# Pooled attention followed by four experts: the first batch's scores by halves of the tokens, chunk 0 written out anew, batch 1 turned by TensorE

## The chip, the cores and the metric

The kernel runs on one core of one Trainium2 chip. The metric is the device time of one execution in microseconds. Six runs of the kernel before are given with their median, and one further trace shows where its time goes, instruction by instruction.

## The reference

Eight batches of eight heads, 576 tokens, head width 64. Keys and values are first averaged over groups of eight tokens (72 pooled keys); every query attends to the 72. The eight heads of a token, side by side, are a row of 512 numbers; 4608 such rows go through four experts of hidden width 1024, whose outputs are added with weights that depend on the row.

```python
k_p = k.reshape(B, H, Sp, pool, D).mean(axis=3)      # pool = 8, Sp = 72
v_p = v.reshape(B, H, Sp, pool, D).mean(axis=3)
attn = softmax(q @ k_p.T / sqrt(D))
x = (attn @ v_p).transpose(0, 2, 1, 3).reshape(B * S, H * D)
p = domain_probs / domain_probs.sum(-1)
for e in range(4):
    out += p[:, e:e+1] * (relu(x @ w1[e]) @ w2[e])
```

## The kernel before

**Chunks.** Every batch gives one chunk of 512 tokens (chunks 0 to 7); the last 64 tokens of all eight batches make chunk 8 (`rem_*`). Chunk 0 is multiplied plainly: `up` (L446) makes hidden blocks `fc` 0 to 7 of an expert, and experts 1 and 2 go down by `down_plain` (L599), expert 0 by `down`. All chunks after it use a scheme with seven products in place of eight for both layers: `up_product` (L493, seven steps for each of two halves, "units") and `down` (L561, seven steps). It needs sums of weights (`first_weight_sums` for w1, `weight_sums` for w2), of inputs (`x_sum`) and of hidden blocks (`hidden_sums`), all made by VectorE through `combine` (L187).

**Order.** Every engine runs its instructions in the order in which the program states them; nothing is reordered. From chunk 1 on a loop runs over slots g. In a slot stand one step of `up_product` for unit 0, the step before it for unit 1, and one step of `down` for the expert before; seven slots make one expert of one chunk. The pieces of attention for the next batch (`fold_keys`, `queries`, `keys`, `scores`, `context`, `turn`), its loads and its `x_sum` pieces stand at slots written by hand in `pieces_later` (L714); for batch 2, slots 0 to 27 run under chunk 1, for batch 3 slots 28 to 55 under chunk 2. Batch 1's pieces stand in `pieces_first` (L681), between the blocks of chunk 0. Where TensorE has nothing to do early on, `idle` (L252) issues matmuls on zeros.

**Loads.** `load_part` brings a quarter of a batch's keys and values at a time and adds it to the quarters before it in memory (L115), `load_whole` brings everything (batches 0 and 1), `load_q` the queries. Most loads are issued by GpSimd and converted on the way, so they queue behind each other on GpSimd and on its DMA queue (q0); an issue also waits for the landing of the load eight issues before it. The queries of batch 0 come as two plain loads from SyncE (queue q1, L132) into `acc`, and VectorE and ScalarE convert them (L136). GpSimd also adds one product of `down` to `acc` for experts 1 to 3 (L592, step 4 of `down`).

**Turning.** What attention gives has tokens on partitions; the experts need the 512 features there. `turn` (L338) does this for 128 tokens at a time: for batch 0 by four TensorE transposes and a ScalarE copy out of PSUM (L348, L349), for all others by a DMA transpose from SyncE's queue (L344). Queries and keys of batches 0 and 1 are turned by TensorE (L285, L233), later ones by DMA (L277, L227).

**PSUM.** `att` and `att_first` are pairs of banks for attention, taken in turn; `unit10` and `unit11` hold hidden blocks; `o_ps0` and `o_ps1` hold the products of `down`. An access to a bank by one engine waits for the access of another engine to the same bank that stands before it in the program.

**Last expert.** `down_last` (L623) makes four quarters of the output in four banks, each of two blocks of 128 tokens; `add` (L642) multiplies a block by its weight and adds it to `acc`, and `store` sends a quarter.

Of the kernel before, what the change touches and what calls it, by code (L numbers as in the profile page):

```python
# [12 lines left out]
BF16 = mybir.dt.bfloat16  # L13
# [4 lines left out]
def kernel(  # L18
# [57 lines left out]
    gate_at = const.tile([1, NR], BF16, name="gate")  # L76
# [27 lines left out]
    def load_whole(b, src, nm):  # L104

        room = wt_bf[:, 1:E].rearrange("p e s i d -> p (e s i d)")
        at = {"kraw": 0, "vraw": 1}[nm] * H * POOL * D
        raw = room[0:SP, at:at + H * POOL * D].rearrange("j (h r d) -> j h r d", h=H, r=POOL)
        for hs in groups(b):
            nc.gpsimd.dma_start(  # L110
                out=raw[:, hs], in_=src[b, hs].rearrange("h (j r) d -> j h r d", r=POOL)
            )
        raws[(nm, b)] = raw
# [9 lines left out]
    def load_q(b):  # L123
        q_sb = raws[("q", b)] = qpool.tile([P, H, NR, D], BF16, name="q_sb")
        src = q[b, :, 0:NT, :].rearrange("h (p r) d -> p h (r d)", r=NR)
        if b:
            nc.gpsimd.dma_start(out=q_sb[:].rearrange("p h r d -> p h (r d)"), in_=src)
            return

        wide = acc[:].rearrange("p r (g t) -> p (r g) t", t=NR * D)  # L130
        for hs in groups(b):
            nc.sync.dma_start(out=wide[:, hs], in_=src[:, hs])  # L132
        for pair in range(NPAIR):
# [110 lines left out]
    def sum_keys(hs):  # L244
        kp = sum_pool(raws[("kraw", 0)], hs)
        nc.vector.tensor_copy(out=kp_all[0:SP, hs, 0, :], in_=kp)
        nc.scalar.copy(out=kp_all[0:SP, hs, 1, :], in_=kp)
# [24 lines left out]
    def queries(b, pair=0):  # L272
# [9 lines left out]
        qt_ps = one_bank(b).bitcast(BF16)[:, 0:4 * P].rearrange("p (h a t) -> p h a t", h=2, a=2)  # L282
# [5 lines left out]
        nc.vector.tensor_copy(out=state[("qT", b)][:, 2 * pair:2 * pair + 2], in_=qt_ps)  # L288
# [49 lines left out]
    def turn(b, r):  # L338
# [4 lines left out]
        if b:  # L343
            nc.sync.dma_start_transpose(out=dst, in_=x_tok)  # L344
            return
        xt_ps = chains[0][:].bitcast(BF16)[:, 0:KC * P].rearrange("p (k t) -> p k t", t=P)
        for kc in range(KC):
            nc.tensor.transpose(xt_ps[:, kc, :], x_tok[:, kc * P:(kc + 1) * P], ident[:])  # L348
        nc.scalar.copy(out=dst, in_=xt_ps)  # L349
# [46 lines left out]

    def attention_first():

        lo, hi = groups(0)
        idle(24)  # L400
# [3 lines left out]
        idle(2)  # L404
        keys(0, lo)
        idle(2)
        sum_keys(hi)
        scores(0, 0)
        queries(0, 2)
        queries(0, 3)  # L410
        idle(1)
        scores(0, 1)
        keys(0, hi)
        sum_values(lo)
        scores(0, 2)
        sum_values(hi)
        idle(2)
        scores(0, 3)
        idle(6)
        half = NT // 2  # L420
        context(0, 0)
        context(0, 1)
        idle(3)
        turn(0, 0)
        context(0, 2)
        idle(2)
        turn(0, 1)
        context(0, 3)
        up(0, 0, range(0, 2), slice(0, half))
        turn(0, 2)  # L430
        up(0, 0, range(2, 4), slice(0, half))
        turn(0, 3)
        up(0, 0, range(4, FCH), slice(0, half))
# [189 lines left out]
    def down_last(c, e):  # L623
# [3 lines left out]
        for row in (1, 0):  # L627
            for col in range(2):
                cols = slice(col * HD, (col + 1) * HD)
                ps = banks[2 * row + col][:].rearrange("p (j d) -> p j d", j=BLOCKS)  # L630
                for j in range(BLOCKS):
                    for fc in range(FCH):
                        nc.tensor.matmul(  # L633
                            ps[:, j], lhsT=H_sb[:, fc // HF, row, fc % HF, j * P:(j + 1) * P],
                            rhs=last_weights(fc, col), start=(j == 0 and fc == 0),
                            stop=(fc == FCH - 1), skip_group_check=True,
                        )
                for j in range(BLOCKS):
                    add(ps[:, j], c, e, row * BLOCKS + j, cols, False)
# [37 lines left out]
    def gate():  # L677

        nc.gpsimd.tensor_copy(out=gate_at[:], in_=state[("xT", 1)][0:1, 0, 0:NT:P])

    def pieces_first():  # L681

        at = {}

        def put(s, i, *pieces):
            at.setdefault((s, i), []).extend(pieces)

        def put_each(slots, pieces):
            for slot, piece in zip(slots, pieces, strict=True):
                put(*slot, piece)  # L690

        put(0, 0, *weight_sums(0))
        put_each([(0, i) for i in range(3, 7)], first_weight_sums(0))
        put_each([(2, i) for i in range(4, 8)], first_weight_sums(1))
        put_each([(2, 0), (2, 1), (2, 2), (3, 1)], weight_sums(1))
        put_each([(2, 7), (3, 2), (3, 4), (3, 6)], weight_sums(3))
        put(1, 3, lambda: fold_keys(1, every))
        for pair in range(NPAIR):
            put(1, 2 + pair, lambda pair=pair: queries(1, pair))
        put(1, 6, lambda: keys(1, every))  # L700
        put(1, 7, lambda: scores(1, 0), lambda: fold_values(1, every))
        for pair in range(1, NPAIR):
            put(2, pair - 1, lambda pair=pair: scores(1, pair))
        for r in range(NR):
            put(2, 3 + r, lambda r=r: context(1, r))
            put(2, 4 + r, lambda r=r: turn(1, r))
        put(3, 1, gate, lambda: load_part(2, 1))
        put(3, 2, lambda: load_q(2))
        put(3, 4, lambda: load_part(2, 2))
        put(3, 6, lambda: load_part(2, 3), lambda: load_q_rem(2))  # L710
        put(3, 7, *(lambda n=n: x_sum(1, n) for n in range(4)))
        return at

    def pieces_later():  # L714
# [7 lines left out]
        for b in range(2, B + 1):  # L722
            start = 7 * E * (b - 2)
            if b < B:
                q_at, k_at, scores_at, contexts_at, loads_at = (
                    (4, 10, (14, 15, 16, 17), (18, 19, 20, 22), (12, 14, 13, 16, 19)) if b == 2
# [6 lines left out]
                for r, slot in enumerate(contexts_at):  # L733
                    put(start + slot, lambda b=b, r=r: context(b, r))
                    put(start + slot + 1, lambda b=b, r=r: turn(b, r))
            if b + 1 < B:
# [5 lines left out]
            if b % 2 == 0:  # L742
                i = b // 2 - 1
                put(start if b == 2 else start - 3, lambda i=i: rem_queries(i))
# [121 lines left out]
```

The softmax here doesn't subtract the row's maximum and nothing guards it: scores larger than these inputs give would overflow.

## Time and profile before

| what | value |
|---|---|
| median of 6 runs | 507.36 us (506.25 to 509.07) |
| profiled execution, its own time | 506.25 us |
| its span on the core | 504.1 us (2.15 us lie around it) |
| instructions | 11277, of them 4580 matmuls |
| TensorE matmul busy | 493.2 us (98%) |
| VectorE busy | 377.6 us (75%) |
| ScalarE busy | 300.6 us (60%) |
| GpSimd busy | 119.9 us (24%) |
| HBM read, written | 45.69 MB, 9.44 MB |
| granted TensorE clock | 0.999 |

All times in the text are microseconds from the start of the span, or durations. "Idle" in a row is the engine's wait before the first instruction of that row, with what ended it. A matmul's end is modelled, so the distance from one start to the next says more than its own length: with 256 columns that is 0.109 us, with 512 columns 0.216 us. Slot 0 starts at 73.24 us, and a slot without a piece of attention takes 1.75 us.

### The profile page before, as it was taken

To read this page: it belongs to the slowest core of one execution; us is meant where nothing else is said; L and a number is where in the kernel's file an instruction comes from. 1 tells how busy PE (TensorE), PEld (TensorE's weight loads), DVE (VectorE), ACT (ScalarE), POOL (GpSimd) and SP (SyncE) were. 2 spreads that over 40 slices of the span, in tenths; PEclk is the share of its full clock that TensorE was granted. 3 is DMA by queue.
4 is the path that set the end of the run, shared out by engine and by line. 5 is a ranking of instruction groups with operands and counts; after the bars stand their busy time and mean duration, and the time that the engine had idled before them with its cause. 6 is when DMAs were issued, how large, how long until landed. Compare 5 with 4: busy or idle time off the path is not lost.

```text
span 504.1 us, 11277 instructions
## 1 busy us (share of the span) xinstructions
PE 493.2 (98%) x4580; PEld 406.8 (81%) x4580; DVE 377.6 (75%) x742; ACT 300.6 (60%) x558; POOL 119.9 (24%) x113
## 2 busy tenths in 40 slices
PE   8999999999899999999999999999999999999995
PEld 4657448878789887888788878888888888888885
DVE  3465689987977887788787868787787767876773
ACT  2665616675576557755665576656755566556650
POOL 6331033462560145112531244010001110111010
PEclk9999999999999999999999999999999999999999
DMA  9999979999599048923793179730310010003003
GB/s 188 209 206 208 201 69 126 152 90 125 62 119 144 1 52 111 131 55 36 68 166 57 27 76 142 61 56 22 85 34 1 22 64 1 12 21 85 1 1 85
DMA packets 106787, 42.48 MB, mean 84 GB/s; under 512 B 79840, under 2 KB 105184, under 8 KB 106736
## 3 DMA queue, kind: packets, MB, share of 16 engines
q0 software_dynamic: 59728, 22.43, 41.3%
q1 hardware_dynamic: 46432, 18.82, 19.6%
q8 instruction: 36, 0.59, 0.5%
q10 hardware_dynamic: 576, 0.52, 0.3%
q14 instruction: 15, 0.12, 0.1%
HBM read 45.69 MB, written 9.44 MB: 109 GB/s over the span
## 4 chain that ended last, share of the span: by engine, by line
PE 92%; DVE 4%; DMA 1%; ACT 1%; issue 1%; DVEq 0%; POOL 0%; ACTq 0%; POOLq 0%
PE o_ps L578 39%; PE unit L510 37%; PE unit L453 5%; PE o_ps L604 3%; PE att L304 2%; DVE S L187 1%; DMA wt_bf<-in_k_dram 1%; PE unit L633 1%; DVE acc L649 1%; PE att L330 1%; PE unit L240 1%; DVE H L491 1%; PE unit L256 1%; ACT o_ps L586 1%; PE o_ps L453 0%
## 5 line engine op out<-in xcount | busy, mean ns | idle before, releaser
L649 DVE SCALAR_TENSOR_TENSOR acc<-o_ps,p_all,acc 128x256 f32<-128x256 f32 (+1 forms) x284 | 126.4, 486 | 57.0 <-PE o_ps L578 39.7
L578 PEld LDWEIGHTS <-H 128*128 128x128 bf16 x1320 | 129.1, 98 | 18.0 <-issue 2.0
L510 PEld LDWEIGHTS <-w_bf 128*128 128x128 bf16 x1024 | 98.0, 98 | 17.5 <-issue 5.8
L491 DVE CUSTOM_DVE_ANT_0 H<-unit,partial 128x512 bf16<-128x512 f32 x128 | 87.7, 686 | 22.9 <-PE unit L510 16.5
L578 PE MATMUL o_ps<-w_bf,H 128*128 128x256 bf16 x792 | 102.6, 272 | 0.9 <-ACT o_ps L586 0.8
L510 PE MATMUL unit<-xT,w_bf 128*128 128x256 bf16 x672 | 96.3, 273 | 0.8 <-ACT unit L523 0.6
L592 POOL TENSOR_TENSOR acc<-acc,addend 128x512 f32<-128x512 f32 x24 | 34.0, 1415 | 262.7 <-ACT addend L590 255.4
L525 ACT COPY partial<-unit 128x512 f32<-128x512 f32 x128 | 72.0, 590 | 31.3 <-PE unit L510 30.8
L510 PEld LDWEIGHTS <-wu_bf 128*128 128x128 bf16 x768 | 73.1, 98 | 10.8 <-issue 2.5
L510 PE MATMUL unit<-xs,wu_bf 128*128 128x256 bf16 x512 | 76.9, 273 | 0.0
L578 PE MATMUL o_ps<-wt_bf,H 128*128 128x256 bf16 x528 | 68.4, 273 | 0.0
L578 PEld LDWEIGHTS <-S 128*128 128x128 bf16 x528 | 51.7, 98 | 6.4
L523 ACT COPY unit<-unit 128x512 f32<-128x512 f32 x64 | 37.3, 582 | 30.7 <-PE unit L510 26.2
L527 ACT ACTIVATE H<-unit 128x512 bf16<-128x512 f32 x64 | 38.8, 606 | 27.6 <-PE unit L510 27.6
L531 ACT ACTIVATE H<-unit 128x512 bf16<-128x512 f32 x64 | 38.1, 596 | 28.2 <-PE unit L510 27.9
L510 PE MATMUL unit<-xs,w_bf 128*128 128x256 bf16 x256 | 38.5, 273 | 1.6 <-DVE H L491 1.5
L647 ACT ACTIVATE acc<-o_ps,p_all 128x256 f32<-128x256 f32 x72 | 30.2, 471 | 13.6 <-PE o_ps L578 10.7
L119 POOL DMA_DIRECT2D kraw<-in_k_dram x18 | 25.3, 1406 | 39.4 <-DMA kraw<-in_k_dram 38.5
L578 PE MATMUL o_ps<-wt_bf,S 128*128 128x256 bf16 x264 | 34.2, 273 | 0.0
L578 PE MATMUL o_ps<-w_bf,S 128*128 128x256 bf16 x264 | 34.2, 273 | 0.0
L510 PE MATMUL unit<-xT,wu_bf 128*128 128x256 bf16 x224 | 33.7, 273 | 0.0
L308 ACT ACTIVATE expT<-att 72x1024 bf16<-72x1024 f32 x28 | 28.6, 1020 | 7.8 <-PE att L304 7.8
(112 smaller groups left out, 524.7 us busy)
## 6 DMA issues: line engine op xcount, KB each, us to landing
out_dram<-acc SPq DMA_DIRECT2D x32, 256.0 KB, 3.4
w_bf<-in_moe_w_dram POOLq DMA_DIRECT2D x7, 1024.0 KB, 22.7
q_sb<-in_q_dram POOLq DMA_DIRECT2D x7, 512.0 KB, 10.9
kraw<-in_k_dram POOLq DMA_DIRECT2D x24, 144.0 KB, 5.8
vraw<-in_v_dram POOLq DMA_DIRECT2D x24, 144.0 KB, 6.8
acc<-in_q_dram SPq DMA_DIRECT2D x2, 512.0 KB, 4.8
w_bf<-in_moe_w_dram POOLq DMA_DIRECT2D x2, 512.0 KB, 11.9
wt_bf<-in_k_dram POOLq DMA_DIRECT2D x2, 288.0 KB, 7.5
```

What stands on the lines that cost most here:

```text
L119: nc.gpsimd.dma_start(out=raw[:], in_=rows, accum_op=ALU.add)
L308: nc.scalar.activation(out=expT[:, 2 * pair:2 * pair + 2].rearrange("j h a b t -> j b (h a) t"), in_=sc_ps[0:SP].rearrange("j b h (a t) -> ...
L491: nc.vector._custom_dve(TENSOR_ADD_SAT, out=dst, in0=ps, in1=part, s0=LARGEST, s1=0.0)
L510: nc.tensor.matmul(ps[:, n * HN:(n + 1) * HN], lhsT=lhs[:, kc, f:f + P], rhs=rhs[:, kc, :], start=(not grows and n == 0 and kc == 0), stop ...
L523: nc.scalar.copy(out=units[unit][1][:], in_=ps)
L525: nc.scalar.copy(out=part[:, step - 2], in_=ps)
L527: nc.scalar.activation(out=quarter(0, 0), in_=ps, func=ACT.Relu)
L531: nc.scalar.activation(out=quarter(0, 1), in_=ps, func=ACT.Relu)
L578: nc.tensor.matmul(ps[:, j], lhsT=lhs[:, i, j * P:(j + 1) * P], rhs=rhs[:, i, :], start=(not grows and i == 0 and j == 0), stop=(i == HF - 1),
L592: nc.gpsimd.tensor_add(out=dst, in0=dst, in1=addend[:])
L647: nc.scalar.activation(out=dst, in_=o_ps, func=ACT.Copy, scale=prob)
L649: nc.vector.scalar_tensor_tensor(out=dst, in0=o_ps, scalar=prob, in1=dst, op0=ALU.mult, op1=ALU.add,)
```

## The change

**Head.** Only the first four heads' queries come from SyncE; the other four come converted on GpSimd's queue, between the keys and the values. Two instructions copy the pooled keys as before, but each now writes both copies of half of the heads. Scores of batch 0 are made for four heads and two of the four token groups at a time (`scores_first`), not for two heads and all tokens, so that the exponentials for the first 256 tokens come first. The order of the head is written out anew with 25 matmuls on zeros in place of 42. `turn(0, 1)` follows `turn(0, 0)` at once, with its own bank and VectorE for the copy; the contexts of the last 256 tokens and their turns stand between expert 0's first blocks.

**Chunk 0.** `first_chunk` replaces `pieces_first` and its loop. Expert 1's and 2's blocks come first with no attention among them (and with the sums for w1 of experts 0 and 1); batch 1's attention stands under expert 3's blocks and the plain `down` products. Batch 1 is turned by TensorE (16 transposes and four ScalarE copies) and no longer by DMA, and `gate`, a GpSimd copy that waited for those DMA transposes, goes.

**Loads.** w1 of experts 2 and 3 moves ahead of w2 of experts 0 and 1 respectively; batch 2's first two parts and its queries are issued ahead of `load_q_rem`, its last two parts at slots 2 and 5.

**Slots.** Under chunk 1, batch 2's queries move from slot 4 to 5, its keys' fold from 10 to 9, its scores from 14..17 to 13..16, its contexts from 18, 19, 20, 22 to 17, 18, 20, 21 (each turn one slot later); the remainder's steps from 0, 5, 9, 10 to 4, 10, 12, 13; batch 3's loads are spread over slots 11 to 25 (12 to 19 before). Under chunk 2, batch 3's queries and fold move from slot 24 to 28 and 29, its contexts from 36, 37, 39, 41 to 43, 44, 46, 47, and its `x_sum` pieces from 44, 44, 48, 51 to 51, 51, 52, 53.

**Last expert.** The two blocks of the very last quarter get a bank each.

```diff
-    def load_q(b):
+    def load_q(b, group=None):
+        hs = groups(b)[group or 0]
+        if group != 0:
+            nc.gpsimd.dma_start(out=q_sb[:, hs]..., in_=src[:, hs])
             return
-        for hs in groups(b):
-            nc.sync.dma_start(out=wide[:, hs], in_=src[:, hs])
-        for pair in range(NPAIR):
+        nc.sync.dma_start(out=wide, in_=src[:, hs])
+        for pair in range(NPAIR // 2):
...
     def sum_keys(hs):
         kp = sum_pool(raws[("kraw", 0)], hs)
-        nc.vector.tensor_copy(out=kp_all[0:SP, hs, 0, :], in_=kp)
-        nc.scalar.copy(out=kp_all[0:SP, hs, 1, :], in_=kp)
+        for i, copy in enumerate((nc.vector.tensor_copy, nc.scalar.copy)):
+            part = slice(i * n, (i + 1) * n)
+            copy(out=kp_all[0:SP, hs][:, part], in_=kp[:, part]...to_broadcast([SP, n, 2, D]))
...
+        bank = one_bank(b) if b else att[:, 0] if pair == 2 else chains[(pair + 1) % 2][:]
...
+        copy = nc.scalar.copy if b == 0 and pair % 2 else nc.vector.tensor_copy
...
     def turn(b, r):
-        if b:
+        if b >= BUSY:
             nc.sync.dma_start_transpose(out=dst, in_=x_tok)
             return
-        xt_ps = chains[0][:]...
+        xt_ps = (one_bank(b) if b else chains[r == 1][:])...
...
-        nc.scalar.copy(out=dst, in_=xt_ps)
+        copy = nc.vector.tensor_copy if (b, r) == (0, 1) else nc.scalar.copy
+        copy(out=dst, in_=xt_ps)
...
+    def scores_first(group, tok):
+        hs = groups(0)[group]
+        sc_ps = two_banks(0)[:].rearrange("p a (h n) -> p a h n", n=P)
+        for hh in range(H // 2):
+            h = hs.start + hh
+            for r2 in range(2):
+                lo = r2 * D
+                nc.tensor.matmul(sc_ps[:, r2, hh], lhsT=key_columns(0, h, lo),
+                                 rhs=qT[lo:lo + D, h, tok], skip_group_check=True)
+        nc.scalar.activation(out=expT[:, hs, tok]..., in_=sc_ps[0:SP], func=ACT.Exp, scale=EXP_SCALE)
...
     def attention_first():
-        idle(24)
-        sum_keys(lo)
-        queries(0, 0)
-        queries(0, 1)
-        idle(2)
-        keys(0, lo)
-        idle(2)
-        sum_keys(hi)
-        scores(0, 0)
-        queries(0, 2)
-        queries(0, 3)
-        idle(1)
-        scores(0, 1)
-        keys(0, hi)
-        sum_values(lo)
-        scores(0, 2)
-        sum_values(hi)
-        idle(2)
-        scores(0, 3)
-        idle(6)
-        context(0, 0)
-        context(0, 1)
-        idle(3)
-        turn(0, 0)
-        context(0, 2)
-        idle(2)
-        turn(0, 1)
-        context(0, 3)
-        up(0, 0, range(0, 2), slice(0, half))
-        turn(0, 2)
-        up(0, 0, range(2, 4), slice(0, half))
-        turn(0, 3)
-        up(0, 0, range(4, FCH), slice(0, half))
+        idle(18)
+        sum_keys(lo)
+        queries(0, 0)
+        queries(0, 1)
+        sum_keys(hi)
+        keys(0, lo)
+        queries(0, 2)
+        queries(0, 3)
+        scores_first(0, 0)
+        keys(0, hi)
+        idle(2)
+        scores_first(1, 0)
+        sum_values(lo)
+        scores_first(0, 1)
+        sum_values(hi)
+        scores_first(1, 1)
+        idle(2)
+        context(0, 0)
+        context(0, 1)
+        idle(2)
+        turn(0, 0)
+        idle(1)
+        turn(0, 1)
+        up(0, 0, range(0, 2), slice(0, half))
+        context(0, 2)
+        up(0, 0, range(2, 3), slice(0, half))
+        context(0, 3)
+        up(0, 0, range(3, 5), slice(0, half))
+        turn(0, 2)
+        up(0, 0, range(5, 7), slice(0, half))
+        turn(0, 3)
+        up(0, 0, range(7, FCH), slice(0, half))
         up(0, 0, range(FCH), slice(half, NT))
...
+    def first_chunk():
...
+        sums = {e: first_weight_sums(e) for e in range(2)}
+        for i in range(FCH):
+            up(0, 1, (i,))
+            if i in (2, 4):
+                hidden_sums(0, 0, i // 2 - 1)
+            if i >= 4:
+                sums[0][i - 4]()
+        for i in range(FCH):
+            up(0, 2, (i,))
+            if i == 1:
+                open_bank(chains[1][:])
+                each(*weight_sums(0))
+            if i >= 2:
+                down(0, 0, i - 2)
+                if i in (3, 4):
+                    hidden_sums(0, 0, i - 1)
+                if i >= 4:
+                    sums[1][i - 4]()
+        down(0, 0, 6)
+        up(0, 3, (0, 1))
+        fold_keys(1, every)
+        up(0, 3, (2,))
+        queries(1, 0)
+        queries(1, 1)
+        up(0, 3, (3,))
+        queries(1, 2)
+        queries(1, 3)
+        up(0, 3, (4,))
+        keys(1, every)
+        up(0, 3, (5,))
+        scores(1, 0)
+        up(0, 3, (6,))
+        scores(1, 1)
+        up(0, 3, (7,))
+        scores(1, 2)
+        fold_values(1, every)
+        down_plain(0, 1, 0)
+        scores(1, 3)
+        down_plain(0, 1, 1)
+        context(1, 0)
+        down_plain(0, 1, 2)
+        context(1, 1)
+        turn(1, 0)
+        down_plain(0, 1, 3)
+        context(1, 2)
+        turn(1, 1)
+        each(*weight_sums(1)[0:2])
+        down_plain(0, 2, 0)
+        context(1, 3)
+        turn(1, 2)
+        each(*weight_sums(1)[2:3])
+        down_plain(0, 2, 1)
+        turn(1, 3)
+        each(*weight_sums(3)[0:2])
+        down_plain(0, 2, 2)
+        each(*(lambda n=n: x_sum(1, n) for n in range(4)))
...
-        for at, pieces in (((2, 2, 3, 4), first_weight_sums(2)), ((14, 14, 16, 16), weight_sums(2)),
+        for at, pieces in (((4, 2), weight_sums(3)[2:]), ((3, 5, 6, 9), first_weight_sums(2)), ((9,), weight_sums(1)[3:]), ((14, 14, 16, 16), weight_sums(2)),
                            ((9, 9, 10, 13), first_weight_sums(3))):
...
     def down_last(c, e):
+                both = [banks[2 * row + col]] * BLOCKS
+                if not row and col:
+                    both[1] = chains[0]
```

## The prediction, made before the changed kernel was run

> **What bounds the kernel now.** I read the page's busy times and chain first, then TensorE's waits, then the timeline of the first 140 us and of the tail.
>
> ```profile
> PE 493.2 (98%) x4580; PEld 406.8 (81%) x4580; DVE 377.6 (75%) x742; ACT 300.6 (60%) x558; POOL 119.9 (24%) x113
> PE 92%; DVE 4%; DMA 1%; ACT 1%; issue 1%; DVEq 0%; POOL 0%; ACTq 0%; POOLq 0%
> ```
>
> TensorE is the bound: a transpose added costs its full time, and a gain can only come from its waits: the head before the first useful block, the few waits after it, the tail.
>
> ```profile
> 0.74 1.01 SPq L132 DMA_DIRECT2D acc<-in_q_dram  x2
> 8.60 1.03 PE L240 MATMUL unit<-wt_bf,ident 72*72 72x256 bf16 x8 [0.17 <-DMA wt_bf<-in_k_dram]
> 10.12 0.37 ACT L247 CAST kp<-unit 72x256 bf16<-72x256 f32 x1 [2.71 <-DVE kp L246]
> 16.81 1.02 ACT L308 ACTIVATE expT<-att 72x1024 bf16<-72x1024 f32 x1 [0.73 <-PE att L304]
> 21.65 0.60 PE L453 MATMUL unit<-xT,w_bf 128*128 128x256 bf16 x4 [0.41 <-ACT xT L349]
> 29.73 7.07 PE L453 MATMUL unit<-xT,w_bf 128*128 128x512 bf16 x32 [0.47 <-ACT H L458]
> ...
> 85.01 1.38 POOL L119 DMA_DIRECT2D kraw<-in_k_dram  x1 [3.30 <-DMA kraw<-in_k_dram]
> 89.69 2.55 DVE L187 TENSOR_TENSOR S<-H,S 128x1024 bf16<-128x1024 bf16 x1
> 89.83 1.85 POOL L592 TENSOR_TENSOR acc<-acc,addend 128x512 f32<-128x512 f32 x1
> 96.80 0.68 DVE L491 CUSTOM_DVE_ANT_0 H<-unit,partial 128x512 bf16<-128x512 f32 x1
> 97.67 0.60 PE L510 MATMUL unit<-xs,w_bf 128*128 128x256 bf16 x4
> ...
> 119.56 1.20 SPq L344 DMA_TRANSPOSE xT<-x_tok  x1
> 124.94 0.43 DVE L187 TENSOR_TENSOR xs<-xT 128x512 bf16<-128x512 bf16 x1 [2.38 <-DMA xT<-x_tok]
> 126.68 0.60 PE L510 MATMUL unit<-xs,w_bf 128*128 128x256 bf16 x4 [1.54 <-DVE H L491]
> 131.13 1.03 PE L510 MATMUL unit<-xT,w_bf 128*128 128x256 bf16 x8 [0.60 <-ACT unit L523]
> ...
> 499.00 0.88 DVE L649 SCALAR_TENSOR_TENSOR acc<-unit,p_all,acc 128x256 f32<-128x256 f32 x2 [0.87 <-PE unit L633]
> ```
>
> These timeline rows show the places the change touches: the head starts with the keys' landing (8.60) and reaches the first block at 21.65; expert 1 starts at 29.73; batch 2's input sums wait 2.38 for a DMA transpose and TensorE then waits for VectorE; the last two adds run together after the last matmul. From 29.73 to slot 0 TensorE's work adds up without a wait: 24 blocks of 0.867 (20.8), seven `down_plain` of 1.735 (12.15), seven steps of `down` (6.1), attention and openings (4.3), together 43.3, and 73.02 - 29.73 is 43.3.
>
> ```profile
> 74.00:100.00 26.00, 25.78 (x254) 21.92 (x252) 25.21 (x47) 15.91 (x31) 11.22 (x10) 1.00 1.11 132
> ```
>
> ```profile
> q1 hardware_dynamic: 820, 0.82, 106.1%
> ```
>
> The stretch table (columns: length, then busy PE, PEld, DVE, ACT, POOL) shows VectorE full, 25.21 of 26 us, under the first seven-product expert. The line under it is from the queue table of 3.0 to 5.2 us: q1 alone moves data, 0.82 MB in 2.2 us, and the keys' queue q0, whose first load was issued at 1.37, has nothing.
>
> **Head.** One of the two 0.52 MB loads leaves q1: at 0.37 MB per us that frees 1.4 us, so I put the first keys at 7.2 in place of 8.56. Bounds: 0 if GpSimd's queue would not have been ready before 5.2, and 1.84 (the two loads' casts start at 4.95 and 6.79). The 18 zero matmuls end at 6.95 (the first nine at 0.425, then 0.216). The rest by rows: sum of half the keys 0.87, a pair's transposes 0.22, VectorE's cast 0.42 with ScalarE's 0.37 after it (it still waits for VectorE: same bank), exponential 1.02, 0.2 from matmul to reader. Second keys land at 9.05 (10.44 less 1.4), and the queries behind them at 10.4 (half of what 0.52 MB takes in this queue, 2.5). TensorE: keys 7.2 to 8.07, two query pairs to 8.52, second keys 9.1 to 9.97, first keys turned and two query pairs to 10.9, scores from 11.0 (VectorE's copy of the keys), second keys turned at 11.7 (ScalarE's copy of the last query pair holds `o_ps0`), their scores from 12.55, values (12.5 and 13.3, as now) and the other scores to 15.6. Exponentials end at 12.7, 14.2, 15.5 and 16.8. The first context starts at 16.05, but the second takes the bank `att`, which the fourth exponential frees at 16.8: the halves are not free of each other. Context to 17.15, VectorE 17.55 to 18.5, turn to 18.8, VectorE's copy to 19.4: first block at 19.45, 2.2 earlier.
>
> Most of that is given back. With contexts and turns among them, blocks 0 to 7 of the first half end at 24.05. ScalarE is full from 22.4 on: relu 0.38 to 0.41 each and two turns' copies of 0.58, the last ending at 24.7. Only block 7 stands behind the last turn (blocks 4 to 7 before), so TensorE waits 0.7. Eight blocks of 0.437 end at 28.25, and the wait of 0.64 before expert 1 (one bank used twice) stays: 28.9 against 29.73, **-0.8**; bounds -1.3 and +0.6.
>
> **Chunk 0.** The 16 transposes of batch 1 cost 0.23 per four (22.52 to 22.75 in the trace): **+0.9**. Their ScalarE copies (4 x 0.58) lie beside `down_plain`s of 1.73. The second two query pairs wait for VectorE, whose queue holds `fold_keys` (1.21 + 0.69 + 0.76) just before: 0.1 and 0.25 by my times, **+0.35**, bounds 0 and 1.0. The moved loads stay off the path: each 1 MB takes about 5.2 in the queue, so w2 of expert 0 lands near 34.1 (needed 37.6), w1 of expert 3 near 39 (49), batch 1's keys near 41.5 (50), w2 of experts 1 to 3 near 52, 57, 62 (58, 67, 71); batch 2's queries pass `load_q_rem`, wanted only at slot 4. Slot 0 thus starts 0.45 later than now.
>
> **Slots 0 to 13** (times from slot 0). The wait at 77.8 (0.39, VectorE's add before ScalarE's copy into `o_ps1`) goes, as the input sums now stand before that add's bank is wanted: **-0.35**, bounds -0.4 and 0. At slot 9 VectorE gets two more weight sums (0.65 each) but loses the remainder's division (0.9) to slot 12. Its run from the fold to the relu of slot 11 (two folds, five weight sums, a hidden sum, `fold_values`, relu) takes 5.5. It starts when the batch's last keys land: GpSimd issues them after its add of slot 5, ending at 13.4, and a load takes 5.8 (the page's median; single ones 3.9 to 7.8), so 19.2, and VectorE is there at 18.6 to 19.7. The relu ends at 24.7 to 25.2; TensorE wants it at 24.1 (in the trace it ended 0.2 ahead: 97.48, 97.67). Then adds, division and the first scores, which share bank `att`: 0.6 more, where five slots lay between before. Sum 1.2 to 1.7 (0.6 to 1.1 at the relu, 0.6 at the scores); what TensorE waits at the first it need not wait again in full at the second, so I take **+1.0**, nearest to the median load; bounds 0 and 3.
>
> In this stretch GpSimd's add (12.0) meets a weight sum of VectorE. The row nearest is 89.69: begun 0.14 ahead of the add, the sum took 2.55 in place of 0.68, and the add 1.85 in place of 1.27 (301.21 and 195.73 are alike; relu and add rows beside it keep their length). The Trainium skill, "SBUF — State Buffer", section "Who interferes with whom", says that a VectorE instruction with two SBUF inputs and a GpSimd one that reads SBUF exclude each other and that the second to start waits. The trace agrees that they collide but shows the first one lengthened too; by the page a sum that starts first would cost VectorE nothing and the stretch would cost 0.5 less.
>
> **Batch 2.** The last turn goes out one slot earlier (issue 117.5 for 119.56), the queries of batch 3 load ahead of the turns and batch 3's fold leaves slot 24. At the same 5.3 to landing this is 122.8, and VectorE asks at 122.56. Start to start TensorE loses 1.71 (124.10 + 0.87 to 126.68), 0.21, 0.76 and 0.15 (at 129.07, 131.13, 133.90) beyond its work: **-2.8**, bounds -2.9 and 0. What is late next is the fold at slot 29: its last part is issued near 120, lands near 126, and is asked for near 129.
>
> **Batch 3 and 4.** Input sums, fold of keys and values now meet in slots 51 to 53: 2.9 of VectorE beside its usual 81%, 1.9 late at the relu, which has 2.0 spare: **+0.2**, bounds 0 and 1.
>
> **Tail.** The first add now runs while the second block is multiplied in its own bank: **-0.4**, half of 0.88.
>
> **Sum:** -0.8 + 0.9 + 0.35 - 0.35 + 1.0 - 2.8 + 0.2 - 0.4 = -1.9. The profiled execution would take 504.35 in place of 506.25. It lies 1.1 under the median of the runs, to which I apply the same difference: **505.5**.
>
> A rule against fewer zero matmuls: "TensorE: Matmul & The Clock Gate", section "What's actually happening", says that about 3.4 us of idling halves the clock. The longest gap I foresee is 0.6 at 8.5, 1.6 if the keys stay at 8.56; no run here shows a re-throttled clock, and by the rule nothing changes.
>
> **Rivals.** *Slower: VectorE is the bound in slots 5 to 14.* It has 0.8 us to spare in 26. If the last keys land 7.8 after an issue delayed by the collision (14.0), the relu ends at 27.3: 3.2 for TensorE, 0.6 for the scores and about 1.2 in the next product, whose copies wait for VectorE: 5 in place of 1, so +2.1, 509.5. It decides against the change from a stretch of 2.9, a landing near 20.7. For it: the full VectorE. Against: less else is loading then. *The queue was not what held the keys:* first keys at 8.56, the head 1.4 worse: -0.5, 506.9. Against: q0's silence until q1 ends. *Batch 2's sums wait as before,* since parts of batch 3 still load under the turns: +0.9, 508.3. For: landings of 8 to 9 us of turns beside loads at 148 us; against: the queries' load, the large one, is done by then.
>
> **How the numbers follow.** A change within 0.3% (1.5 us) is about what a measurement of this kernel cannot tell from none. Forecast 0.55 (faster 0.50, same 0.05), slower rival 0.18 (0.15 slower, 0.03 same), keys rival 0.16 (faster 0.02, same 0.13, slower 0.01), batch 2 rival 0.11 (same 0.08, slower 0.03). Faster 0.52, same 0.29, slower 0.19. The forecast's own range is 503.0 (head at its bound, slots 0 to 13 without a wait, no query waits) to 506.9; upward I go to 509.0, which leaves out the slower rival's upper half.
>
> **What would show it.** First block near 19.4, expert 1 near 28.9, slot 0 near 73.5; TensorE waits of 0.5 to 1.5 between slots 7 and 14; no wait of VectorE for a DMA transpose near 122; one add after the last matmul. Wrong if TensorE waits for VectorE by more than 2.9 before slot 14, if batch 2's wait stays, or if the first keys' sum still starts at 8.6.

## The result, and the profile after

| kernel | median, us | ratio to the kernel before, 95% interval |
|---|---|---|
| before | 507.17 (40 runs) | |
| changed | 513.26 (19 runs) | 1.0109 [1.0086, 1.0132] |

The change makes the kernel 1.1% slower, 5.5 us by the ratio and 6.1 by the medians; the forecast was 505.5 with an upper end of 509.0. The profiled execution of the changed kernel took 513.54, its span 511.8 against 504.1.

The page of the changed kernel, busy times and chain:

```profile
PE 492.7 (96%) x4595; PEld 407.3 (80%) x4595; DVE 373.9 (73%) x740; ACT 302.8 (59%) x562; POOL 120.5 (24%) x113
...
PE 76%; DMA 9%; DVE 9%; ACT 2%; issue 2%; POOL 1%; SPq 0%; DVEq 0%; POOLq 0%; ACTq 0%
```

TensorE is busy no longer than before (492.7 for 493.2), in a span 7.7 longer. On the chain it falls from 92% to 76%, while DMA comes from 1% to 9% and VectorE from 4% to 9%: the loss is waiting, on transfers and on the VectorE work behind them. The timeline of the changed kernel says where. The head first:

```profile
6.74 1.03 PE L242 MATMUL unit<-wt_bf,ident 72*72 72x256 bf16 x8
...
19.14 0.60 PE L481 MATMUL unit<-xT,w_bf 128*128 128x256 bf16 x4 [0.61 <-DVE xT L357]
...
28.18 2.10 PE L481 MATMUL unit<-xT,w_bf 128*128 128x512 bf16 x9 [0.47 <-ACT H L486]
```

The first keys are summed at 6.74 (8.60 before), the first block starts at 19.14 (21.65), expert 1 at 28.18 (29.73), and slot 0 at 72.7 (73.2). Up to slot 12 the changed kernel is 1.2 ahead (94.7 against 95.9). Then, in the same view:

```profile
84.55 0.68 DVE L189 TENSOR_TENSOR wu_bf<-w_bf,wu_bf 128x1024 bf16<-128x1024 bf16 x1
...
84.68 1.68 POOL L620 TENSOR_TENSOR acc<-acc,addend 128x512 f32<-128x512 f32 x1 [10.75 <-DVE H L519]
...
86.31 1.39 POOL L118 DMA_DIRECT2D kraw<-in_k_dram  x1
...
86.89 4.11 SPq L282 DMA_TRANSPOSE qT<-q_sb  x1
...
91.06 3.51 SPq L689 DMA_DIRECT2D out_dram<-acc  x2
...
96.45 0.76 DVE L223 TENSOR_TENSOR kp<-kraw 72x512 bf16<-72x512 bf16 x2 [6.04 <-DMA kraw<-in_k_dram]
...
99.19 0.84 ACT L679 ACTIVATE acc<-o_ps,p_all 128x256 f32<-128x256 f32 x2 [6.35 <-DMA out_dram<-acc]
...
100.08 1.86 PE L606 MATMUL o_ps<-w_bf,S 128*128 128x256 bf16 x8 [4.32 <-ACT acc L679]
...
101.19 1.28 DVE L519 CUSTOM_DVE_ANT_0 H<-unit,partial 128x512 bf16<-128x512 f32 x2
```

GpSimd issues batch 2's last keys at 86.31, directly after its add; SyncE starts the DMA transpose of batch 2's queries 0.6 later and is held by it for 4.1. The keys land at 96.43, 10.1 after their issue, and VectorE has waited 6.04 for them. The stores of chunk 0 stand behind the transpose on SyncE; the one issued at 91.06 lands at 99.10, and ScalarE, which is to overwrite that part of `acc`, has waited 6.35. TensorE stands for 4.48. The stretch table of the changed kernel (length; busy PE, PEld, DVE, ACT, POOL; granted clock, DMA share, GB/s) shows a further cost:

```profile
96.60:100.00 3.40, 0.00 (x0) 0.00 (x0) 3.37 (x7) 0.81 (x3) 0.85 (x1) 1.00 1.04 189
100.00:103.40 3.40, 3.32 (x29) 2.20 (x29) 3.37 (x8) 2.61 (x6) 2.43 (x4) 0.51 0.62 54
```

After 3.4 us without a matmul the granted clock is 0.51 for the next 3.4, in which TensorE is full: 1.7 more, as half of that work is lost. From slot 0 to slot 14 the changed kernel takes 32.4 (72.7 to 105.1) and the kernel before 26.2; 0.42 of the difference is a step of `scores` that now stands ahead of slot 14. By then the changed kernel is 5.7 behind (105.1 against 99.4), of 7.7 at the end.

Two later places and the tail, from the timeline again:

```profile
130.65 0.42 DVE L189 TENSOR_TENSOR xs<-xT 128x512 bf16<-128x512 bf16 x1 [2.48 <-DMA xT<-x_tok]
...
131.73 0.60 PE L538 MATMUL unit<-xs,w_bf 128*128 128x256 bf16 x4 [0.98 <-DVE H L519]
...
176.28 0.69 DVE L326 TENSOR_TENSOR x_tok<-att,inv 128x512 bf16<-128x512 f32 x1 [2.50 <-DMA xT<-x_tok]
...
507.28 0.48 DVE L681 SCALAR_TENSOR_TENSOR acc<-o_ps,p_all,acc 128x256 f32<-128x256 f32 x1 [0.39 <-PE o_ps L664]
```

Batch 2's input sums still wait for a turn by DMA (2.48; before 2.38). A division of batch 3 waits 2.50 for the buffer that an earlier turn still reads, which costs TensorE 1.41 near 177. One add is left after the last matmul, 0.48 in place of 0.88.

### The profile page after: what moved, and what is told of

It reads as the page before. It is cut to its first block, busy times and chain, and to the rows that moved or that the text cites. A ratio compares the mean times of both kernels' runs of the same rounds, so it can differ in the third digit from the quotient of the medians.

```text
span 511.8 us, 11293 instructions
## 1 busy us (share of the span) xinstructions
PE 492.7 (96%) x4595; PEld 407.3 (80%) x4595; DVE 373.9 (73%) x740; ACT 302.8 (59%) x562; POOL 120.5 (24%) x113
## 4 chain that ended last, share of the span: by engine, by line
PE 76%; DMA 9%; DVE 9%; ACT 2%; issue 2%; POOL 1%; SPq 0%; DVEq 0%; POOLq 0%; ACTq 0%
PE o_ps L606 32%; PE unit L538 31%; DMA xT<-x_tok 5%; PE unit L481 5%; DVE acc L681 3%; PE o_ps L632 2%; DMA wt_bf<-in_v_dram 2%; DMA out_dram<-acc 2%; DVE S L189 2%; PE att L311 1%; DVE H L519 1%; DMA kpT<-kp 1%; PE unit L664 1%; DVE x_tok L326 1%; PE att L337 1%
## 5 line engine op out<-in xcount | busy, mean ns | idle before, releaser
L538 PEld LDWEIGHTS <-wu_bf 128*128 128x128 bf16 x768 | 73.2, 98 | 10.8 <-issue 2.3
L679 ACT ACTIVATE acc<-o_ps,p_all 128x256 f32<-128x256 f32 x72 | 30.2, 471 | 18.4 <-PE o_ps L606 10.1
L118 POOL DMA_DIRECT2D vraw<-in_v_dram x18 | 30.1, 1672 | 10.0 <-DMA vraw<-in_v_dram 9.5
```

What stands on the lines that cost most here:

```text
L118: nc.gpsimd.dma_start(out=raw[:], in_=rows, accum_op=ALU.add)
L538: nc.tensor.matmul(ps[:, n * HN:(n + 1) * HN], lhsT=lhs[:, kc, f:f + P], rhs=rhs[:, kc, :], start=(not grows and n == 0 and kc == 0), stop ...
L679: nc.scalar.activation(out=dst, in_=o_ps, func=ACT.Copy, scale=prob)
```

## The experiments

Three theories for the loss near slot 12. *Collision:* the queries' transpose, the loads of the last keys and values and the stores run together and lengthen each other. *Order on GpSimd:* the keys are issued too late, behind the add. *VectorE:* it has too much work there, whatever lands when.

### Queries turned two slots earlier; last keys loaded one slot earlier

Two kernels, each the changed one with one edit:

```diff
-                    (5, 9, (13, 14, 15, 16), ...
+                    (3, 9, (13, 14, 15, 16), ...
```

> The changed kernel with the DMA transpose of batch 2's queries at slot 3 instead of 5, nothing else. Theory of the collision: in the changed kernel the transpose (issued 86.89, landing 97.41), the last keys and values (86.31 to 96.43, 87.17 to 98.16) and the stores behind the transpose on SyncE (91.06 to 99.10) lengthen each other, so TensorE waits 4.48 at 95.49 and then runs at half clock to 103.4. Two slots earlier the transpose should land near 85 to 87, the last keys in 6 to 7, near 92.5, and the stores in 3 to 5; the wait falls under 1, and the time by 4.5 to 6.5 us against the changed kernel: 507 to 509, within 0.4% of the kernel before. Theory that the keys are late because their issue stands behind GpSimd's add: they are still issued at 86.3, so at most 2 us better. Theory that VectorE has simply too much work in slots 5 to 14: under 1 us better.

```diff
-                put(start + 5, lambda: load_part(2, 3), lambda: load_q_rem(2))
+                put(start + 4, lambda: load_part(2, 3))
+                put(start + 5, lambda: load_q_rem(2))
```

> The changed kernel with the loads of the last quarter of batch 2's keys and values at slot 4 instead of 5, which puts them ahead of the add of slot 5 on GpSimd; the transpose of the queries stays at slot 5. GpSimd can then issue them near 78.5 and 80.2, when the quarters before have landed. Theory of the issue behind the add: the keys land near 84 to 85, VectorE never waits for them, the 4.48 wait goes but for what the stores leave of it; 5 to 6.5 us better than the changed kernel, 507 to 508.5. Theory of the collision: the same for the keys, and the transpose, left alone, lands in 5 to 6 in place of 10.5, so that the stores are in time too. If the stores alone decide (ScalarE waits 6.4 for one of them), and they remain behind the transpose, TensorE still waits 2 to 3 near slot 12. Theory of too much VectorE work: under 1 us better.

Measured: 507.39, ratio 0.9999 [0.9974, 1.0024], and 507.49, ratio 1.0007 [0.9979, 1.0034]. Each edit alone gives back the whole loss, so too much work of VectorE by itself is out. In the first, the keys are issued behind the add as before and land in 6.0 (90.88 to 96.85; this execution is 4.5 late from its head on, see below), so lateness of the issue alone is out too: it takes the late issue and the transpose beside it. Why the two lengthen each other no run here shows. The timeline of the first:

```profile
84.55 3.64 SPq L282 DMA_TRANSPOSE qT<-q_sb  x1
...
90.88 1.39 POOL L118 DMA_DIRECT2D kraw<-in_k_dram  x1
...
96.87 0.76 DVE L223 TENSOR_TENSOR kp<-kraw 72x512 bf16<-72x512 bf16 x2 [1.91 <-DMA kraw<-in_k_dram]
```

The second, in the timeline of its trace:

```profile
79.76 1.38 POOL L118 DMA_DIRECT2D kraw<-in_k_dram  x1 [5.80 <-DMA kraw<-in_k_dram]
...
87.25 3.54 SPq L282 DMA_TRANSPOSE qT<-q_sb  x1
...
90.69 0.74 DVE L223 TENSOR_TENSOR kp<-kraw 72x512 bf16<-72x512 bf16 x2
...
93.36 0.84 ACT L679 ACTIVATE acc<-o_ps,p_all 128x256 f32<-128x256 f32 x2 [0.16 <-DMA out_dram<-acc]
```

The keys go out at 79.76 and land at 86.16, before the transpose begins; that, now with only the small load of `q_rem` (64 KB) beside most of it, lands in 5.1 in place of 10.5, the stores behind it in 2.4 to 2.6 in place of 8.0 and 6.4. Of the waits for them 0.16 of ScalarE is left.

### Which of the two late transfers set the wait

The chain of waits of the changed kernel goes through the store and not through the keys:

```profile
91.06 8.05 DMA out_dram<-acc
...
99.56 0.48 ACT acc L679
...
100.08 1.86 PE o_ps L606 x8
```

Two kernels leave stores of chunk 0 out, all four in one and the last two in the other:

```diff
-        if e == E - 1 and step in (1, 4, 5, 6):
+        if c and e == E - 1 and step in (1, 4, 5, 6):
```

```diff
-        if e == E - 1 and step in (1, 4, 5, 6):
+        if e == E - 1 and step in ((1, 4, 5, 6) if c else (1, 4)):
```

> The changed kernel without the stores of chunk 0 (its four quarters are not written out; all else as it is). The chain of waits names the store that was issued at 91.06 behind the queries' transpose and landed at 99.10: ScalarE waits 6.4 for it and TensorE for ScalarE. If this store alone sets the wait near slot 12, it falls under 1 and the kernel gets 4.5 to 6 us faster, 507 to 509. If VectorE's wait for the last keys (to 96.43) is as late by itself, its relus still end at 101.9 and not before, and slot 13 starts near 102 in place of 102.5: under 1.5 us faster, 512 to 513.5, the idle time standing behind another wait.

Measured: 506.66, ratio 0.999 [0.9966, 1.0015]. Both predicted outcomes are about stores, but the cause here is another: with no store ahead of it on SyncE the transpose went out at 77.99 and was done at 83.99, and the keys landed in 5.1 (86.40 to 91.54). It is the first experiment again, and says nothing on the store.

> The changed kernel without the last two of chunk 0's four stores (those issued at 91.06 and 93.49; these two quarters are not written out). The first two stay, so that SyncE still reaches the queries' transpose at 86.9, beside the loads of the last keys: leaving out all four let it go at 78.0, so that the keys landed in 5.1 and the question was not answered. Store alone: no engine waits for it any more, the wait near slot 12 falls under 1.5, 507 to 509. Keys as late by themselves: the keys land near 96, VectorE's relus end near 101.5, slot 13 starts near 102 and slot 14 is at most 1 earlier than 105.1: 512 to 513.5.

Measured: 513.16, ratio 1.0125 [1.0094, 1.0157]: as slow as the changed kernel. Without the store that the chain named nothing is gained. The timeline:

```profile
85.12 1.68 POOL L620 TENSOR_TENSOR acc<-acc,addend 128x512 f32<-128x512 f32 x1 [11.25 <-DVE H L519]
...
96.64 0.76 DVE L223 TENSOR_TENSOR kp<-kraw 72x512 bf16<-72x512 bf16 x2 [5.80 <-DMA kraw<-in_k_dram]
...
102.12 1.01 PE L538 MATMUL unit<-xs,w_bf 128*128 128x256 bf16 x4 [4.67 <-DVE H L519]
```

The keys land at 96.62 (9.9 after their issue). VectorE needs 5.5 from there to its relus, and TensorE now waits 4.67 for them, two steps further on. Two waits lay over each other, and the chain shows only the one that TensorE meets first: in the changed kernel the relu was done at 101.87, while TensorE was still busy with the steps that the store had held.

### The orders alone, in the kernel before

The kernel before, with `load_part(2, 2)` at slot 2, `load_part(2, 3)` and `load_q_rem(2)` at slot 5 (taken out of `pieces_first`), and:

```diff
-                    (4, 10, (14, 15, 16, 17), ...
+                    (5, 10, (14, 15, 16, 17), ...
```

> The kernel before with three things of the change alone: the third quarter of batch 2's keys and values loaded at slot 2, the last at slot 5 (behind GpSimd's add), and its queries turned at slot 5 in place of 4. The fold stays at slot 10. If these orders by themselves make the loss: last keys issued near 86 to 87, landing 9 to 11 later at 96 to 98, a TensorE wait of 3 to 5 near slot 12, half clock after it: 511.5 to 514, slower than the kernel before by 4 to 6.5 us. If it takes the new chunk 0, the new slots of the fold (9) or the moved weight sums as well: under 2 us slower.

Measured: 509.32, ratio 1.0055 [1.0023, 1.0087], between the two forecasts.

```profile
86.89 1.39 POOL L119 DMA_DIRECT2D kraw<-in_k_dram  x1
...
87.44 4.28 SPq L277 DMA_TRANSPOSE qT<-q_sb  x1
...
96.38 0.76 DVE L221 TENSOR_TENSOR kp<-kraw 72x512 bf16<-72x512 bf16 x2 [0.95 <-DMA kraw<-in_k_dram]
...
98.68 0.84 ACT L647 ACTIVATE acc<-o_ps,p_all 128x256 f32<-128x256 f32 x2 [4.50 <-DMA out_dram<-acc]
...
99.57 1.53 PE L578 MATMUL o_ps<-w_bf,S 128*128 128x256 bf16 x8 [2.57 <-ACT acc L647]
```

The same picture: keys 9.5 to landing beside the transpose, TensorE idle. But the fold stands a slot later, so VectorE had work until 95.4 and waited only 0.95 for the keys. Here it is the store behind the transpose that holds TensorE: ScalarE waits 4.50 for it, and TensorE 2.57 for ScalarE. So the store is late enough to cost time too; in the changed kernel it was hidden by keys that were as late. After this shorter wait the clock falls as well: from 96.5 to 99.9 TensorE is busy for 0.83, and in the next 3.4 the granted clock is 0.51.

From slot 0 to 14 this execution takes 30.6, 4.4 more than before and 1.8 less than the changed one; 0.9 of that comes back at batch 2's sums, which wait less, and 2.15 is lost again at 166.58. It took 513.48 in all, against a median of 509.32, so its places do not add up to the measured difference of 0.55%. The faster half of the executions has a mean granted clock of 0.997 or more, the slower half 0.991 to 0.996. Of the 1.8, 0.42 is the step of `scores`; that the rest belongs to the fold's earlier slot and the two weight sums behind it (1.3) is argued, not shown apart.

### Head, chunk 0 and tail without the new slots

The changed kernel with the tables of the kernel before from slot 0 on; and the run with the keys at slot 4 with batch 3's old slots and loads:

```diff
-                    (5, 9, (13, 14, 15, 16), (17, 18, 20, 21), (11, 12, 14, 22, 25)) if b == 2
-                    else (0, 1, (6, 10, 11, 12), (15, 16, 18, 19), (4, 17, 7, 10, 13)) if b == 3
+                    (5, 9, (13, 14, 15, 16), (17, 18, 20, 21), (12, 14, 13, 16, 19)) if b == 2
...
-            for n, slot in enumerate((24, 25, 25, 26) if b == 2 else (23, 23, 24, 25) if b == 3
-                                     else (16, 16, 20, 23) if b < B
+            for n, slot in enumerate((24, 25, 25, 26) if b == 2 else (16, 16, 20, 23) if b < B
```

> Head, chunk 0 with its TensorE turns, and tail as in the changed kernel; the pieces of attention and their loads from slot 0 on as in the kernel before (the weight sums moved into slots 2 to 9 stay moved). What head, chunk 0 and tail are worth together: slot 0 began at 72.7 against 73.2 and the tail after the last matmul took 4.8 against 5.36, so by the traces 1.1 us faster than the kernel before if the slots run as before, 505.5 to 507. If the turning by DMA in the kernel before had spared something in the slots, or the moved weight sums clog VectorE in slots 2 to 9, it comes out 1 to 2 slower instead.

> As the run with the keys at slot 4, and batch 3's queries, fold, contexts and input sums at the slots of the kernel before, with the loads of batch 3 at slots 12, 14, 13, 16, 19 in place of 11, 12, 14, 22, 25. The traces put the new slots of batch 3 at 0.93 (keys of batch 3 landing at 147.95, wanted at 147.07) plus 1.41 (wait near 177 for a division that waits for a DMA transpose of 9.3), and batch 2's waits near 130 to 136 at 2.5. Theory that loads under the turns cost this: all three shrink, 1.5 to 4 us better than the run with the keys at slot 4 alone. If the waits come from elsewhere, within 1 of it.

Measured: 505.38, ratio 0.9976 [0.995, 1.0002], and 505.14, ratio 0.9975 [0.9945, 1.0005]. Both lie where the forecasts put them, but neither interval excludes no gain. In the second, batch 3's waits of 0.93 and 1.41 are gone, while batch 2's stay at 1.45 and 0.76, as batch 3's last two quarters of keys and values still lie under batch 2's turns. By the medians the new head, chunk 0 and tail are worth about what the traces say, 1 to 2 us; clear of the noise that is not shown.

### No load beside a turn

```diff
-                    (5, 9, (13, 14, 15, 16), (17, 18, 20, 21), (11, 12, 14, 22, 25)) if b == 2
-                    else (0, 1, (6, 10, 11, 12), (15, 16, 18, 19), (4, 17, 7, 10, 13)) if b == 3
+                    (5, 9, (13, 14, 15, 16), (17, 18, 20, 21), (11, 12, 14, 16, 26)) if b == 2
+                    else (0, 3, (7, 10, 11, 12), (15, 16, 18, 19), (4, 17, 7, 10, 13)) if b == 3
```

> As the run with the keys at slot 4, with nothing loaded under batch 2's four turns: batch 3's third quarter at slot 16 (ahead of them) and the last at slot 26 (behind GpSimd's add of that slot, so that it cannot be issued early) in place of 22 and 25, which both go out at 114.6 since GpSimd runs ahead to its add of slot 19. Batch 3's fold goes from slot 29 to 31, its first scores from 34 to 35. Theory of loads under the turns: the last two turns land in 2.4 to 3 in place of 8.5 and 6.0, and the waits of 0.96, 0.95 and 0.28 between 124.9 and 130.6 go: 2 us faster than the run with the keys at slot 4, 505 to 506. If the turns are slow whatever else moves, the same within 0.7. Risk: the last keys land late for the fold at slot 31, which would cost up to 3.

Measured: 506.44, ratio 0.998 [0.9952, 1.0009]; runs from 503.15 to 509.05. The last two turns of batch 2 land in 2.5 and 3.7 (8.5 and 6.0 with the keys at slot 4 alone), and the waits near 125 to 131 are gone. The load now lies beside the first two turns (6.8 and 5.0 for 2.5), where TensorE does not come to wait. Another has grown in their place, in the timeline of this run:

```profile
122.09 0.42 DVE L189 TENSOR_TENSOR xs<-xT 128x512 bf16<-128x512 bf16 x1
...
167.72 0.69 DVE L326 TENSOR_TENSOR x_tok<-att,inv 128x512 bf16<-128x512 f32 x1 [3.34 <-DMA xT<-x_tok]
...
169.72 1.03 PE L538 MATMUL unit<-xT,w_bf 128*128 128x256 bf16 x8 [2.09 <-ACT unit L551]
```

The load of batch 4's queries was issued at 155.1, beside batch 3's turns. One number more puts it behind GpSimd's add of slot 47:

```diff
-                    else (0, 3, (7, 10, 11, 12), (15, 16, 18, 19), (4, 17, 7, 10, 13)) if b == 3
+                    else (0, 3, (7, 10, 11, 12), (15, 16, 18, 19), (4, 19, 7, 10, 13)) if b == 3
```

> As the run turns_free, with the load of batch 4's queries at slot 47 in place of 45, which puts it behind GpSimd's add of that slot and so behind batch 3's turns. In turns_free the load went out at 155.1 beside the four turns (157.5 to 169.6), the division of the fourth token group waited 3.34 for a transpose, and TensorE 2.25 at 167.35. Theory of loads beside transposes: that wait goes and the turns land in 2.5 to 5; 1.5 to 2.3 us faster than turns_free, 504 to 505, the fastest so far. If something else holds the turns there (batch 4's last quarter of keys, 151 to 160), under 0.7 faster. A late landing of the queries (wanted at slot 59) should not matter: 12 slots lie between.

Measured: **502.64, ratio 0.992 [0.9899, 0.994]**, faster than both kernels, with runs from 501.62 to 503.38. It was expected to gain 1.5 to 2.3 on turns_free and gained 3.8 by the medians. Part of that is the clock: six of the 12 executions of turns_free have a mean granted clock of 0.997 or less and took 507.14 to 509.05, the six others 503.15 to 505.75; all six of this kernel have 0.998 or more. Against the six others alone the gain is about 1.7, inside what was expected; that the load's slot also keeps the clock up is not shown. Its timeline:

```profile
165.37 0.69 DVE L326 TENSOR_TENSOR x_tok<-att,inv 128x512 bf16<-128x512 f32 x1
...
167.05 0.96 POOL L129 DMA_DIRECT2D q_sb<-in_q_dram  x1
```

The division no longer waits, and the turns land in 4.4, 2.4, 2.4 and 2.4. Its span is 501.2.

### The head without its zero matmuls

The profiled execution of the run with the queries at slot 3 was the slowest of its runs (511.51, where the median is 507.39), with slot 0 at 77.2 in place of 72.7. Its stretch table:

```profile
8.10:11.50 3.40, 2.09 (x26) 1.83 (x25) 1.39 (x4) 1.22 (x3) 1.25 (x2) 1.00 1.27 190
11.50:14.90 3.40, 3.27 (x32) 1.84 (x31) 0.73 (x2) 1.86 (x3) 1.87 (x3) 0.53 1.28 200
```

The queries of the last four heads landed at 11.30 (9.80 in the changed kernel's trace), and the clock stayed at half until 22. To see how near the edge the new head is, the kernel with batch 3's old slots lost its seven zeros after the first 18:

```diff
         keys(0, hi)
-        idle(2)
         scores_first(1, 0)
...
         scores_first(1, 1)
-        idle(2)
         context(0, 0)
         context(0, 1)
-        idle(2)
         turn(0, 0)
-        idle(1)
         turn(0, 1)
```

> As the run with the keys at slot 4 and batch 3's old slots (505.1), without the seven zero matmuls that the new head issues between its first 18 and its first block. One profiled execution of the run with the queries at slot 3 had the granted clock at 0.50 from 12 to 22 us, and its slot 0 began 4.2 later, though no gap of TensorE was longer than 0.82. Theory of the clock: with the zeros gone the share of busy time falls further and the clock drops in most executions: 3 to 5 us slower, 508 to 510. Theory that the zeros only fill waits: 504.5 to 505.5, and the profiled head keeps its clock at 1.00.

Measured: 509.26, ratio 1.0023 [0.9995, 1.0051], against 505.14 with the zeros. Stretches of it:

```profile
13.60:17.00 3.40, 2.73 (x42) 1.94 (x41) 1.75 (x4) 2.24 (x3) 1.70 (x3) 1.00 1.24 210
17.00:20.40 3.40, 2.34 (x14) 1.53 (x15) 1.32 (x3) 0.66 (x2) 0.94 (x2) 0.50 1.14 212
```

The clock is half from 17.0 to 23.8, and the kernel pays about 4. All 12 of its executions have a mean granted clock of 0.993 or less; with the zeros 10 of 12 have 0.998 or more. So the zeros hold the clock. The share of busy time by itself does not tell: the changed kernel kept its clock after 2.53 of 3.40 busy (9.2 to 12.6), and this one lost it after 2.73. What counts as activity no run here shows.

## Why the prediction was wrong, step by step

**Head: right in mechanism, a little small.** First block 19.45 foreseen, 19.14 measured; expert 1 28.9 foreseen, 28.18 measured: the wait for the last turn's copy is 0.44 and not 0.7, and the blocks before it end 0.4 earlier. The gain is 1.55, not 0.8. The rival by which q1 did not hold the keys is ruled out by the sum at 6.74.

**Chunk 0: right.** From expert 1 to slot 0 the time grows from 43.5 to 44.5: 1.0, where 0.9 + 0.35 stood. Only a wait of 0.25 at 70.0 came with the turns. The wait at 77.8 is gone, as foreseen. (Two slips of the working change nothing: 0.45 after 73.24 is 73.7, not 73.5, and the three bounds named for the low end of the range take 0.5, 1.0 and 0.35 from 505.5, which is 503.6 and not 503.0.)

**Slots 0 to 13: the step that failed.** The chain of the working held: GpSimd's add ended 13.7 after slot 0 (13.4 foreseen), and VectorE needed 5.4 from landing to relu (5.5 foreseen). What failed is the load time between them: "a load takes 5.8 (the page's median; single ones 3.9 to 7.8)". It took 10.1, since the moved transpose of the queries ran beside it, and the term of +1.0 became 4.5 of idling and 1.7 of half clock. The text moved the keys' fold, the loads and the transpose past each other, but counted the load at a median over all stretches, and did not ask what q1 would carry in that one. The slower rival had the place and the deciding point (a landing 20.7 after slot 0; it was 23.8). It did not have the cause: it blamed VectorE's full load, which two experiments rule out by itself, and its price of 2.1 was capped at a load of 7.8.

**Half clock.** The Trainium skill, "TensorE: Matmul & The Clock Gate", section "What's actually happening", was held against the head alone, with the words that nothing changes by it. (That no run had shown a halved clock holds but for the tail of the trace before, 0.50 from 503.4 on, behind the last matmul.) It should have been held against the slower rival: a wait near 4.5 is longer than the page's 3.4, and the 0.51 after it agrees with the page. But the runs also show that less is enough. The clock fell to half after 3.4 us with 0.25 (no_last_stores_chunk0, 97.2 to 100.6), 0.51 (old_slots, 125.1 to 128.5) and 0.83 busy (before_late_keys), and the longest wait in the last was 2.57, so the rival's own 3.2 could already have cost clock. For the head the page and the runs differ more: by its table it takes an idle window, but head_no_zeros lost the clock with no gap of TensorE over 0.64 and 2.73 of 3.40 us busy, and queries_slot3 with none over 0.82 and 2.09 busy. The measurement decides: thinning the zeros was a risk that the working put at nothing.

**Batch 2: -2.8 foreseen, -0.3 measured.** The waits were 2.8 and are 2.5 (1.15, 0.95, 0.28, 0.15). The rival "wait as before" was right, and right in its reason. The forecast assumed the transpose's 5.3 and said that the large load was done by then; the third quarter of batch 3's keys was issued at 120.23, between the second turn and the third, and these turns took 8.4 and 6.2. With no load issued under them (turns_free) the wait was gone, as the term had it.

**Batch 3 and 4: +0.2 foreseen, about 2.3 measured** (0.93 for keys that land at 147.95, 1.41 for the division). The step looked at VectorE's load, and the waits came from transposes of 6.3 and 9.3 beside loads; a further 1.2 at 273.8 has the same division as its cause. It does not show at that place in the trace before.

**VectorE against GpSimd.** The +1.0 counted on a weight sum lengthened by GpSimd's add, from the row at 89.69 of the trace before. In the changed kernel the sum at 84.55 kept its 0.68 and the add, begun 0.13 later, took 1.68; at 132.71 a sum begun 0.07 after an add took 1.49 in place of 0.42. Both agree with the Trainium skill, "SBUF — State Buffer", section "Who interferes with whom", by which the second to start waits; the old row remains the exception.

**Tail: right.** From the start of the last matmuls to the end 5.37 became 4.80: 0.57, where 0.4 stood.

## What to carry to other kernels

Price a transfer in the stretch where it will run, with everything that the changed order puts beside it, and not at its median: here a load and a DMA transpose that met took up to twice as long as apart. Where an engine runs ahead, a load's slot means only "behind the last instruction that held that engine", so an order is moved by moving it past such an instruction. A chain of waits shows one late thing per place; before mending it, ask what else is late there, and count the clock with any wait like the 2.6 us that halved it here.

## What the runs showed of the hardware

- A quarter of the keys (144 KB, issued by GpSimd) landed in 10.1, 9.9 and 9.5 where the DMA transpose of the queries was issued 0.55 to 0.58 behind it, and in 9.3 where it was 1.2 behind; with the transpose out of the way in 5.1 to 7.0. The transpose itself took 10.0 to 12.1 beside the load and 5.0 to 6.0 where the loads of keys and values were out of its way. In the kernel before, the transpose was issued 1.0 ahead of the load, and the load took 6.6.
- A turn of 128 tokens landed in 2.4 to 2.5 alone and in up to 10.1 beside a load: in the changed kernel 8.4 and 6.2 for batch 2's last two and 9.3 for batch 3's first, in turns_free 10.1 for batch 3's first.
- The granted clock fell to half after 3.4 us in which TensorE was busy for 0, 0.25, 0.51 or 0.83 us (longest waits 4.5 down to 2.6), and stayed full after 3.4 us with 1.62 busy (before_late_keys, 164.8 to 168.2). In the head it also fell with TensorE 61% and 80% busy by the profile in the 3.4 us ahead and no gap of a microsecond, while 74% kept it.
